# Load figures of a list scheduler, and the place from which it counts sums that need ScalarE's last copy

## The chip, the core and the metric

The kernel runs on one core of a Trainium2 chip. The time is device time of one launch in microseconds. The core's engines work side by side: TensorE (PE; its weight loads are listed as PEld), VectorE (DVE), ScalarE (ACT), GpSimd (POOL) and SyncE (SP, which issues most transfers). Each engine takes its instructions in the order in which the program emits them, and waits where an operand isn't ready or a buffer isn't free. The order of emission is therefore the schedule.

## The reference

Two blocks follow one another. The first is a gated linear recurrence over 768 steps, for 4 batches of 8 heads with head size 48:

```
f = 1 / (1 + exp(-f_logit))
for t in range(768):
    state = f[t][:, None] * state + outer(k[t], v[t])
    y[t] = q[t] @ state
```

The second takes its result as 3072 tokens of 384 channels through a bilinear layer: `((x @ w_a) * (x @ w_b)) @ w_out`, with 1536 columns in `w_a` and `w_b`. Everything is float32; the weights arrive as 64-bit numbers and are converted on the chip.

## The kernel before

**Units and blocks.** The attention is cut into 16 units: a batch, a half of the sequence (384 steps), and four heads. Two units make one block of 384 tokens (8 blocks, numbered 0 to 7). A unit's *front* (`front_parts`) prepares its inputs: two sigmoids on ScalarE (`opposite`, `sigmoid`), `affine` on POOL, and on VectorE two long scans (`scan_f`), two tiny operations (`hold`, `restart`), six short scans (`scan_inv`) and two products (`times`). Its *core* (`core_parts`) is matmuls on TensorE (`scores`, `turn`, `gains`, `within`, `across`), with `mask`, `carry` and `hand_on` on VectorE and `turned` and `out_of_bank` on ScalarE between them. The result is stored into a block's `xT` by transfers.

**The bilinear layer.** Blocks 0 and 1 use plain products (`up`: 12 chunks per block, each of 6 matmuls called beats; `product` multiplies the two halves). Blocks 2 to 7 use a scheme with fewer products over sums of weights and of `xT`: `up_triples` runs four rounds `j` of 15 products in each block. Each product of a round takes one beat on TensorE and is written to one of four PSUM banks (`ps_f`). ScalarE's `copy` or VectorE's `add` takes it out, and the bank is then used again. The third argument of `on` is the number of beats after which that happens, the *due*. In a round VectorE also does two longer sums over earlier copies (into `c[:, :, 1:3, 1]` from `first`, into `c[:, :, 0]` from `second`), and in `finish` the product of the two factors. `down` then multiplies pairs of token groups with `w_out`: 21 beats per pair. `combine_x` makes a block's sums of `xT`.

**The order up to some 111 us** is written out by hand: fronts and cores of units 0 to 3, the weights' conversion, and the first 19 chunks of `up`, which count beats as they are emitted (`on_pe`). Here the load figures play no role.

**From there a list scheduler** emits everything. `main` is a fixed list: the last ten chunks of `up`, then `down` and `up_triples` block by block. Each entry names its engine, a load in ns and a due. Beside it stand six *lines* of work in a fixed order each: sums of `w_out`, sums of `xT` (`for_x`), the attention's core, its fronts, its loads, and sums of the other weights. Before each entry of `main`, `fill` puts in whatever steps of the lines fit. It keeps a planned time `now` for TensorE and `free_at` for the other engines. A step on TensorE fits when its inputs are ready by `now`; a step on another engine when its planned start is at most one BEAT ahead of `now` and `delays` doesn't object:

```
start = max(start, free_at[engine])
fits = start <= now + BEAT and not delays(engine, start, load)
```

`delays` walks through the next 80 entries of `main` and is to say whether the step would make one of them miss its due beat. `starts` holds the planned starts of the coming beats, by a count (`beats_done`) that begins at zero with `main`; the dues were made with `beats[0]`. After a filler, `free_at[engine]` (or `now`) moves by its load. After an entry of `main` on another engine it becomes `max(free_at, now + 200) + load`.

Other limits: `across` of a new block waits in the list until the block two before it is through (`past`), since there are two `xT`; a stored unit counts as landed after 5000 ns, a load after 6000.

Of the kernel before, what the change touches and what calls it, by code (L numbers as in the profile page):

```python
# [133 lines left out]
def by_quotients(ctx, tc, q, k, f_logit, v, moe_w_a, moe_w_b, moe_w_out, out, ident, weights, bad):  # L134
# [156 lines left out]
    def front_parts(u):  # L291

        t = sets[u % NSET]
        x = halves(t["f"])
        F = halves(products_of_f[u])
        inv = invs[u % 2 if u < 2 * NQ else 0]
        none = zero.broadcast_to((128, BLK))
        got = {}

        def sigmoid():  # L300
            nc.scalar.activation(F, x, AF.Sigmoid)

        def opposite():
            nc.scalar.activation(inv, x, AF.Sigmoid, bias=less, scale=-1.0, accum_out=tails[:, u:u + 1])  # L304

        def affine():
            nc.gpsimd.tensor_scalar(inv, inv, EXP_K, 1.0, ALU.mult, ALU.add)  # L307

        def scan_f(n):
            c = slice(n * BLK, n * BLK + BLK)  # L310
            nc.vector.tensor_tensor_scan(F[:, c], F[:, c], none, math.exp(MIDDLE), ALU.mult, ALU.add)  # L311

        def hold():
            nc.vector.tensor_tensor(held[:, u], products_of_f[u][:, :, BLK - 1], least, ALU.is_ge)

        def restart():
            got["start"] = sb2.tile([128, 2, NC - 1], FP32, tag="start", name="start")
            by_chunk = products_of_f[u].rearrange("p n (c m) -> p n c m", m=C)
            nc.vector.reciprocal(got["start"], by_chunk[:, :, 0:NC - 1, C - 1])

        def scan_inv(n, c):
            w = slice(n * BLK + c * C, n * BLK + c * C + C)
            first = got["start"][:, n, c - 1:c] if c else math.exp(-MIDDLE)
            nc.vector.tensor_tensor_scan(inv[:, w], inv[:, w], none[:, 0:C], first, ALU.mult, ALU.add)  # L324

        def times(nm, by):
            live.setdefault(u, {})
            nc.vector.tensor_tensor(halves(t[nm]), halves(t[nm]), by, ALU.mult)

        first = ((ACT, 980, opposite), (ACT, 850, sigmoid))  # L330
        return (
            [*(first[::-1] if u in FIRST else first), (POOL, 1000, affine)],
            [(DVE, 870, scan_f, 0), (DVE, 870, scan_f, 1), (DVE, 160, hold)],
            [(DVE, 170, restart), *((DVE, 410, scan_inv, n, c) for n in range(2) for c in range(NC))],
            [(DVE, 880, times, "q", F), (DVE, 880, times, "k", inv)],
        )

# [222 lines left out]
        return groups[:, first:first + NTG].rearrange("p g (k t) -> p g k t", k=NFT)  # L560


    BEAT = 4 * 164
    ISSUE = 430
    beats = [0]

    def on_pe(load, do, *args):
        beats[0] += 1
        return PE, load, 0, do, *args

    def on(engine, load, due, do, *args):
        return engine, load, beats[0] + due if due else 1 << 30, do, *args

    factors = []

# [120 lines left out]
        write(b22, b22, -1)  # L696
        yield

    X_STEPS = [(DVE, 480)] + [(DVE, 270)] * 10 + [(ACT, 350)]

    def add_steps(to, x, y, op=ALU.add):
        nc.vector.tensor_tensor(to, x, y, op)  # L702
# [1 line left out]
    def up_triples(blk):  # L704
# [15 lines left out]
            return on_pe(BEAT, emit, ps, name, j, start)  # L720

        def copy(due, x, ps):
            return on(ACT, 490, due, nc.scalar.copy, x, ps)

        def finish(j, c, out, v):
            yield times(v, "v6", j)
            yield copy(5, out[1, 0], v)
            a, b = (
                c[:, g].rearrange("p k i t -> p k (i t)").rearrange("p k (g t) -> p g k t", g=NTG) for g in range(2)
            )  # L730
            yield on(DVE, 1280, 0, add_steps, to.rearrange("p g (k j) t -> p j g k t", k=NI)[:, j], a, b, ALU.mult)

        for j in range(NJ3):
            v, u, r, t = (ps_f[i][:, 0:BLK].rearrange("p (g t) -> p g t", g=2) for i in free)
            free[:] = [free[i] for i in ((2, 1, 3, 0) if j < NJ3 - 1 else (2, 3, 1, 0))]
            c = (sums, last[:, 0:2 * NI * BLK])[j % 2].rearrange("p (g k i t) -> p g k i t", g=2, k=NI, i=2)
            out = {(k, i): c[:, :, k, i] for k in range(NI) for i in range(2)}
            if j % 2:
                at = thirds.index(down_first[0])
                pairs = [thirds[(at + n) % 3] for n in (1, 2)]  # L740
            else:
                pairs = [last[:, PIECE * n:PIECE * n + PIECE] for n in range(2)]
            first, second = (x.rearrange("p (g n t) -> p g n t", g=2, n=2) for x in pairs)

            def add(due, k, i, ps):
                return on(DVE, 480, due, add_steps, out[k, i], ps, out[k, i])

            yield times(v, "v1", j, True)
            yield copy(3, out[2, 0], v)
            if tail:  # L750
                yield from finish(*tail)
            yield times(u, "u1", j, True)
            yield copy(3, out[1, 1], u)
            yield times(r, "r2", j, True)
            yield add(6, 1, 1, r)
            yield times(v, "v2", j)
            yield copy(3, out[2, 1], v)
            yield times(u, "u2", j)
            yield copy(3, first[:, :, 1], u)
            yield times(t, "t1", j, True)  # L760
            yield copy(6, out[0, 0], t)
            yield times(v, "v3", j)
            yield copy(3, first[:, :, 0], v)
            yield on(DVE, 880, 0, add_steps, c[:, :, 1:3, 1], c[:, :, 1:3, 1], first)
            yield times(u, "u3", j)
            yield copy(3, out[0, 1], u)
            yield times(r, "r3", j, True)
            yield add(6, 2, 1, r)
            yield times(v, "v4", j)
            yield copy(3, second[:, :, 1], v)  # L770
            yield times(u, "u4", j)
            yield add(3, 0, 0, u)
            yield times(t, "t2", j)
            yield add(5, 0, 1, t)
            yield times(v, "v5", j)
            yield copy(2 if j == NJ3 - 1 else 3, second[:, :, 0], v)
            yield times(u, "u5", j)
            yield add(3, 2, 0, u)
            yield on(DVE, 880, 0, add_steps, c[:, :, 0], c[:, :, 0], second)
            tail = j, c, out, v  # L780
        yield from finish(*tail)

# [2 lines left out]
    def down(pair):  # L785
# [56 lines left out]
            nc.sync.dma_start(out=out[blk * BLK + g * 128:blk * BLK + g * 128 + 128], in_=got["o", i])  # L842

        yield from times(x0, a11, b11, True)
        yield on(ACT, 330, 4, begin)
        s1, s2 = block(), block()
        yield add(10, s1, a21, a22)
        yield add(7, s2, s1, a11, ALU.subtract)
        yield from times(m1, s3, t3, True)
        yield on(ACT, 330, 7, second)  # L850
        yield from times(x0, a12, b21)
        yield on(ACT, 330, 7, third)
        s4 = block()
        yield add(10, s4, a12, s2, ALU.subtract)
        yield from times(x1, s2, t2, True)
# [11 lines left out]
    def core_parts(s):  # L867


        u = s - 1  # L870
        if u < 2 * NQ:
            yield PE, 1150, 0, scores, s, None
        elif s < NU:
            yield PE, 1850, 0, within_and_scores, u
        else:
            yield PE, 1050, 20 * BEAT, within, u
        if s < NU:
            yield DVE, 880, 0, mask, s
            yield PE, 700, 0, turn, s, None
            yield ACT, 850, 0, turned, s  # L880
        if u < 2 * NQ:
            yield PE, 1050, 0, gains, s, False
        elif s < NU:
            yield PE, 1750, 0, gains_and_across, u
        else:
            yield PE, 1050, 0, across, u, False
        if s < NU:
            for j in range(NJ - 1 if unit(s)[1] == NH - 1 else NJ):
                yield DVE, 230, 0, carry, s, j
            if unit(s)[1] < NH - 1:  # L890
                yield DVE, 500, 0, hand_on, s
        if u >= 2 * NQ:
            for part in range(3):
                yield ACT, 490, 0, out_of_bank, u, part
            begin, *stores = stores_of(u)
            yield SP, 0, 0, begin
            for do in stores:
                yield SP, ISSUE, 5000, do

# [33 lines left out]
    with tc.manual_schedule():  # L933
# [187 lines left out]
                    past=behind[blk - 1] if blk > 2 else behind["down"],  # L1121
                )

        LATENCY = 200
        now, free_at, done = 0, [0] * 5, 0

        def earliest(line):
# [8 lines left out]

        def delays(engine, start, load):

            with_it, without = start + load, free_at[engine]
            t, beat = now, beats_done  # L1140
            starts, later = {}, []
            for e, cost, due, *_ in main[done:done + 80]:
                if e == PE:
                    beat += 1
                    starts[beat] = t
                    t += cost
                elif e == engine:
                    later.append((t + LATENCY + (0 if due < 1 << 29 or e != DVE else 600), cost, due))
            for ready, cost, due in later:
                if ready >= with_it:  # L1150
                    return False
                with_it, without = (max(x, ready) + cost for x in (with_it, without))
                if with_it + 500 > max(starts.get(due, 1 << 30), without + 500):
                    return True
            return False

# [40 lines left out]
        for done, (engine, load, due, do, *args) in enumerate(main):  # L1197
# [6 lines left out]
                now += load  # L1204
                beats_done += 1
            else:
                free_at[engine] = max(free_at[engine], now + LATENCY) + load
            do(*args)  # L1208
        done = len(main)
        for line in lines:  # L1210
# [349 lines left out]
```

## Time and profile before

| what | value |
|---|---|
| median of 3 runs | 611.31 us (610.23 to 612.02) |
| profiled execution | 612.79 us, span 611.1 us |
| TensorE busy / its weight loads | 572.6 us (94%) / 511.6 us (84%) |
| VectorE busy | 410.5 us (67%) |
| ScalarE busy | 268.7 us (44%) |
| POOL busy | 76.1 us (12%) |
| mean granted TensorE clock | 0.98 |
| 240 records of products without a stall (one block of triples) | 39.24 us |

The page gives busy time per engine, the span in 40 slices, the chain that ended last, and groups of instructions with busy time, mean duration, and idle time before them with who ended it. A matmul of float32 is recorded twice, so a beat of `up_triples` shows as four records. Reported durations on VectorE and ScalarE overlap: the next instruction on the same engine can start before the reported end of the one before it. In the views of waits a line reads "engine, tile and line, waited for <- whom: us in total, times, longest us". L1208 is the scheduler's own call, under which ScalarE's copies of `main` appear; L702 is `add_steps`.

### The profile page before, as it was taken

Reading aid. Unit: us, or ns where it says so; the run is one execution under the profiler, and the core shown is the slowest. Engines: PE = TensorE matmul, PEld = TensorE weight load, DVE = VectorE, ACT = ScalarE, POOL = GpSimd, SP = SyncE. Lnnn points to the kernel's source line nnn. Section 1 sums busy time; section 2 is a strip of 40 time slices with the busy share of each in tenths; the row PEclk is TensorE's granted clock in tenths of the full one; section 3 lists DMA queues with packets and bytes.
Section 4 is the critical chain, followed back from the end, with each engine's and each line's share of the span. In section 5 each row is a group of like instructions: output and inputs, shape, how many; then the busy total and the mean of one; then the engine's idle time right before and its main releaser. Section 6 shows DMA issues by size and latency. Waiting matters only on the chain.

```text
span 611.1 us, 13867 instructions
## 1 busy us (share of the span) xinstructions
PE 572.6 (94%) x5778; PEld 511.6 (84%) x5778; DVE 410.5 (67%) x762; ACT 268.7 (44%) x508; POOL 76.1 (12%) x69
## 2 busy tenths in 40 slices
PE   0759899999999999999999999999999999999995
PEld 0626555556999999999889998999899999999995
DVE  6778434578987778976897668756776255836741
ACT  5657498963312545335531353326331245235300
POOL 6333154544200000000000000000000000000000
PEclk9859999999999999999999999999999999999998
DMA  9978586139944144034003510023001100000000
GB/s 203 241 213 251 133 268 206 53 58 164 161 124 124 37 88 92 9 106 100 20 2 81 134 34 1 2 73 72 1 3 47 35 11 1 1 27 0 1 28 31
DMA packets 33336, 49.42 MB, mean 81 GB/s; under 512 B 3952, under 2 KB 25072, under 8 KB 33264
## 3 DMA queue, kind: packets, MB, share of 16 engines
q1 hardware_dynamic: 29984, 42.38, 25.6%
q0 software_dynamic: 2992, 5.77, 5.6%
q8 instruction: 47, 0.77, 0.5%
q10 hardware_dynamic: 288, 0.30, 0.2%
q14 instruction: 25, 0.20, 0.1%
HBM read 33.23 MB, written 4.72 MB: 62 GB/s over the span
## 4 chain that ended last, share of the span: by engine, by line
PE 82%; DVE 5%; DMA 5%; ACT 2%; issue 2%; SPq 1%; ACTq 0%; DVEq 0%
PE ps_f L710 32%; PE ps_f L803 27%; PE ps_f L588 15%; DMA xT<-y 2%; PE ps_y L476 2%; PE ps_y L497 2%; PE ps_x L433 2%; PE ps_x L374 1%; DVE groups L702 1%; PE ps_x L409 1%; DMA f_in<-in_f_logit_dram 1%; DVE sums L702 1%; DMA k_in<-in_k_dram 1%; DVE inv L324 1%; DVE f_in L311 1%
## 5 line engine op out<-in xcount | busy, mean ns | idle before, releaser
L588 PE MATMUL ps_f<-xT,w_ba 128*128 128x384 f32 x288 | 99.6, 505 | 7.0 <-DMA xT<-y 3.7
L588 PEld LDWEIGHTS ps_f<-xT,w_ba 128*128 128x128 f32 x288 | 55.1, 195 | 47.0 <-issue 7.4
L1208 ACT COPY sums<-ps_f 128x384 f32<-128x384 f32 x120 | 57.6, 481 | 75.3 <-PE ps_f L710 68.7
L1208 ACT COPY groups<-ps_f 128x384 f32<-128x384 f32 x120 | 57.7, 481 | 68.4 <-PE ps_f L710 47.8
L710 PE MATMUL ps_f<-xT,w_ba 128*128 128x192 f32 x384 | 78.5, 327 | 0.0
L710 PEld LDWEIGHTS ps_f<-xT,w_ba 128*128 128x128 f32 x384 | 64.7, 190 | 0.3
L710 PE MATMUL ps_f<-x_sums,raw 128*128 128x192 f32 x288 | 53.7, 330 | 2.6 <-DVE groups L702 2.0
L710 PE MATMUL ps_f<-groups,w_ba 128*128 128x192 f32 x288 | 55.6, 328 | 0.0
L710 PEld LDWEIGHTS ps_f<-x_sums,raw 128*128 128x128 f32 x288 | 47.0, 190 | 5.5 <-DVE groups L702 3.2
L803 PE MATMUL ps_f<-w_out,groups 128*128 128x192 f32 x288 | 51.6, 328 | 0.0
L803 PE MATMUL ps_f<-w_out,sums 128*128 128x192 f32 x288 | 51.5, 327 | 0.0
L803 PE MATMUL ps_f<-spare,sums 128*128 128x192 f32 x288 | 49.8, 327 | 0.0
L710 PEld LDWEIGHTS ps_f<-groups,w_ba 128*128 128x128 f32 x288 | 47.9, 190 | 0.8 <-ACT sums L1208 0.4
L803 PEld LDWEIGHTS ps_f<-w_out,groups 128*128 128x128 f32 x288 | 47.2, 190 | 0.6
L60 POOL TENSOR_SCALAR sums<-sums 128x768 f32<-128x768 f32 (+1 forms) x20 | 41.3, 2067 | 50.8 <-ACT sums L58 49.0
L803 PEld LDWEIGHTS ps_f<-w_out,sums 128*128 128x128 f32 x288 | 47.4, 190 | 0.2
L702 DVE TENSOR_TENSOR sums<-sums,groups 128x768 f32<-128x768 f32 x36 | 35.3, 980 | 18.0 <-ACT groups L1208 17.6
L803 PEld LDWEIGHTS ps_f<-spare,sums 128*128 128x128 f32 x288 | 47.0, 190 | 0.1
L702 DVE TENSOR_TENSOR sums<-ps_f,sums 128x384 f32<-128x384 f32 x60 | 33.0, 553 | 20.0 <-PE ps_f L710 16.2
L307 POOL TENSOR_SCALAR inv<-inv 128x768 f32<-128x768 f32 x14 | 12.3, 881 | 267.0 <-ACT inv L304 241.4
L710 PE MATMUL ps_f<-x_sums,w_ba 128*128 128x192 f32 x192 | 39.6, 329 | 1.0 <-DVE groups L702 0.5
L710 PE MATMUL ps_f<-xT,raw 128*128 128x192 f32 x192 | 39.8, 330 | 0.2 <-ACT groups L1208 0.2
(123 smaller groups left out, 856.1 us busy)
## 6 DMA issues: line engine op xcount, KB each, us to landing
raw<-w_ba POOLq DMA_DIRECT2D x11, 512.0 KB, 8.2
q_in<-in_q_dram SPq DMA_DIRECT2D x32, 144.0 KB, 4.2
k_in<-in_k_dram SPq DMA_DIRECT2D x32, 144.0 KB, 3.6
v_in<-in_v_dram SPq DMA_DIRECT2D x16, 288.0 KB, 5.0
raw<-in_moe_w_out_dram SPq DMA_DIRECT2D x6, 768.0 KB, 4.2
out_dram<-o SPq DMA_DIRECT2D x24, 192.0 KB, 1.9
f_in<-in_f_logit_dram SPq DMA_DIRECT2D x28, 144.0 KB, 3.0
xT<-y SPq DMA_DIRECT2D x46, 72.0 KB, 2.1
```

The lines of the kernel that those rows point to most:

```text
L60: nc.gpsimd.tensor_scalar(h, h, HI_MAX, None, ALU.min)
L307: nc.gpsimd.tensor_scalar(inv, inv, EXP_K, 1.0, ALU.mult, ALU.add)
L311: nc.vector.tensor_tensor_scan(F[:, c], F[:, c], none, math.exp(MIDDLE), ALU.mult, ALU.add)
L324: nc.vector.tensor_tensor_scan(inv[:, w], inv[:, w], none[:, 0:C], first, ALU.mult, ALU.add)
L433: nc.tensor.matmul(ps_x[R * h:R * h + D, p, (n * NC + c) * D:(n * NC + c) * D + D], lhsT=kT[r, n, c, R * h:R * h + D], rhs=t["v"][r, n, c, ...
L476: nc.tensor.matmul(ps[p][e:e + D, o:o + SUB], lhsT=t["v"][r, n, c, h * D:h * D + D], rhs=at[r, h, o:o + SUB], start=o == 0, stop=True, ski ...
L497: nc.tensor.matmul(ps[p][e:e + D, o:o + SUB], lhsT=st[j][r, n], rhs=qf[r, tokens(n, c, p)], start=False, stop=True, skip_group_check=True,)
L588: nc.tensor.matmul(ps[nm][:, 0:BLK], lhsT=w[:, kt, ft * 128:ft * 128 + 128], rhs=xT[blk][:, kt], start=kt == 0, stop=kt == NKT - 1,)
L702: nc.vector.tensor_tensor(to, x, y, op)
L710: nc.tensor.matmul(ps[:, g], lhsT=sums_of_w[name][:, g, 128 * j:128 * j + 128], rhs=sums_of_x[blk][name], start=start and g == 0, stop=Tru ...
L803: nc.tensor.matmul(to, lhsT=x[:, i // 2, i % 2], rhs=w[:, NI * (i % 2) + i // 2], start=start and i == 0, stop=i == HFT - 1, skip_group_ch ...
L1208: do(*args)
```

## The change

It replaces load figures, and it marks entries of `main` on VectorE that read ScalarE's last copy. The mark adds 8 to the engine's number. For such an entry the main loop counts `free_at` from `last_copy + 200` where that is later than `now + 200`; `last_copy` is the planned end of the last copy emitted from `main` (before, it was set to 0 and not used). `delays` gets the same count for coming entries, in place of 600 ns on VectorE's entries that have no due. No instruction is added or removed, and no instruction's operands change.

```
-        first = ((ACT, 980, opposite), (ACT, 850, sigmoid))
+        first = ((ACT, 930, opposite), (ACT, 750, sigmoid))
-            [*(first[::-1] if u in FIRST else first), (POOL, 1000, affine)],
-            [(DVE, 870, scan_f, 0), (DVE, 870, scan_f, 1), (DVE, 160, hold)],
-            [(DVE, 170, restart), *((DVE, 410, scan_inv, n, c) for n in range(2) for c in range(NC))],
+            [*(first[::-1] if u in FIRST else first), (POOL, 830, affine)],
+            [(DVE, 870, scan_f, 0), (DVE, 870, scan_f, 1), (DVE, 80, hold)],
+            [(DVE, 90, restart), *((DVE, 385, scan_inv, n, c) for n in range(2) for c in range(NC))],
...
-    BEAT = 4 * 164
+    BEAT = 653
+    COPIED = 8
...
-    def on(engine, load, due, do, *args):
-        return engine, load, beats[0] + due if due else 1 << 30, do, *args
+    def on(engine, load, due, do, *args, copied=False):
+        return engine + COPIED * copied, load, beats[0] + due if due else 1 << 30, do, *args
...
-            return on(ACT, 490, due, nc.scalar.copy, x, ps)
+            return on(ACT, 400, due, nc.scalar.copy, x, ps)
...
-            yield on(DVE, 1280, 0, add_steps, to.rearrange("p g (k j) t -> p j g k t", k=NI)[:, j], a, b, ALU.mult)
+            yield on(DVE, 1280, 0, add_steps, to.rearrange("p g (k j) t -> p j g k t", k=NI)[:, j], a, b, ALU.mult, copied=True)
...
-            yield add(6, 1, 1, r)
+            yield add(6, 1, 1, r, True)
...
-            yield on(DVE, 880, 0, add_steps, c[:, :, 1:3, 1], c[:, :, 1:3, 1], first)
+            yield on(DVE, 870, 0, add_steps, c[:, :, 1:3, 1], c[:, :, 1:3, 1], first, copied=True)
...
-            yield on(DVE, 880, 0, add_steps, c[:, :, 0], c[:, :, 0], second)
+            yield on(DVE, 870, 0, add_steps, c[:, :, 0], c[:, :, 0], second, copied=True)
...
-            yield PE, 1850, 0, within_and_scores, u
+            yield PE, 1600, 0, within_and_scores, u
...
-            yield PE, 700, 0, turn, s, None
-            yield ACT, 850, 0, turned, s
+            yield PE, 850, 0, turn, s, None
+            yield ACT, 700, 0, turned, s
...
-            yield PE, 1750, 0, gains_and_across, u
+            yield PE, 1550, 0, gains_and_across, u
...
-                yield DVE, 230, 0, carry, s, j
+                yield DVE, 180, 0, carry, s, j
-                yield DVE, 500, 0, hand_on, s
+                yield DVE, 320, 0, hand_on, s
...
-        LATENCY = 200
+        LATENCY, MARGIN = 200, 500
...
-            with_it, without = start + load, free_at[engine]
+            with_it, without, copied = start + load, free_at[engine], max(free_at[ACT], last_copy)
...
-                elif e == engine:
-                    later.append((t + LATENCY + (0 if due < 1 << 29 or e != DVE else 600), cost, due))
+                    continue
+                ready = t + LATENCY
+                if e >= COPIED:
+                    ready = max(ready, copied + LATENCY)
+                if e == ACT:
+                    copied = max(ready, copied) + cost
+                if e % COPIED == engine:
+                    later.append((ready, cost, due))
...
-                if with_it + 500 > max(starts.get(due, 1 << 30), without + 500):
+                if with_it + MARGIN > max(starts.get(due, 1 << 30), without + MARGIN):
...
-                free_at[engine] = max(free_at[engine], now + LATENCY) + load
+                ready = max(now, last_copy if engine >= COPIED else 0) + LATENCY
+                engine %= COPIED
+                free_at[engine] = max(free_at[engine], ready) + load
+                if engine == ACT:
+                    last_copy = free_at[ACT]
```

Smaller figures change in the same way: `scores`, `within`, `gains` and `across` alone to 1000, adds in the rounds from 480 to 470, three small copies in `down` from 330 to 220, the first and last step of `combine_x` from 480 and 350 to 470 and 270.

More of the change, by code (lines that the diff above doesn't have):

```diff
@@ L697, in combine_x @@
         yield
-    X_STEPS = [(DVE, 480)] + [(DVE, 270)] * 10 + [(ACT, 350)]
+    X_STEPS = [(DVE, 470)] + [(DVE, 270)] * 10 + [(ACT, 270)]
     def add_steps(to, x, y, op=ALU.add):
@@ L743, in up_triples, with add @@
             first, second = (x.rearrange("p (g n t) -> p g n t", g=2, n=2) for x in pairs)
-            def add(due, k, i, ps):
-                return on(DVE, 480, due, add_steps, out[k, i], ps, out[k, i])
+            def add(due, k, i, ps, copied=False):
+                return on(DVE, 470, due, add_steps, out[k, i], ps, out[k, i], copied=copied)
             yield times(v, "v1", j, True)
@@ L844, in down @@
         yield from times(x0, a11, b11, True)
-        yield on(ACT, 330, 4, begin)
+        yield on(ACT, 220, 4, begin)
         s1, s2 = block(), block()
@@ L849, in down @@
         yield from times(m1, s3, t3, True)
-        yield on(ACT, 330, 7, second)
+        yield on(ACT, 220, 7, second)
         yield from times(x0, a12, b21)
-        yield on(ACT, 330, 7, third)
+        yield on(ACT, 220, 7, third)
         s4 = block()
@@ L871, in core_parts @@
         if u < 2 * NQ:
-            yield PE, 1150, 0, scores, s, None
+            yield PE, 1000, 0, scores, s, None
         elif s < NU:
-            yield PE, 1850, 0, within_and_scores, u
+            yield PE, 1600, 0, within_and_scores, u
         else:
-            yield PE, 1050, 20 * BEAT, within, u
+            yield PE, 1000, 20 * BEAT, within, u
         if s < NU:
             yield DVE, 880, 0, mask, s
-            yield PE, 700, 0, turn, s, None
-            yield ACT, 850, 0, turned, s
+            yield PE, 850, 0, turn, s, None
+            yield ACT, 700, 0, turned, s
         if u < 2 * NQ:
-            yield PE, 1050, 0, gains, s, False
+            yield PE, 1000, 0, gains, s, False
         elif s < NU:
-            yield PE, 1750, 0, gains_and_across, u
+            yield PE, 1550, 0, gains_and_across, u
         else:
-            yield PE, 1050, 0, across, u, False
+            yield PE, 1000, 0, across, u, False
         if s < NU:
             for j in range(NJ - 1 if unit(s)[1] == NH - 1 else NJ):
-                yield DVE, 230, 0, carry, s, j
+                yield DVE, 180, 0, carry, s, j
             if unit(s)[1] < NH - 1:
-                yield DVE, 500, 0, hand_on, s
+                yield DVE, 320, 0, hand_on, s
         if u >= 2 * NQ:
```

## The prediction

> **What bounds the kernel now.** I read the page's busy rows first, then its groups, then the table by stretches of 25 us, then the waits of TensorE's weight loads and of VectorE between 195 and 485 us, then the timeline of VectorE around single stalls.
>
> From the page:
>
> ```profile
> PE 572.6 (94%) x5778; PEld 511.6 (84%) x5778; DVE 410.5 (67%) x762; ACT 268.7 (44%) x508; POOL 76.1 (12%) x69
> PE 0759899999999999999999999999999999999995
> ...
> L1208 ACT COPY sums<-ps_f 128x384 f32<-128x384 f32 x120 | 57.6, 481 | 75.3 <-PE ps_f L710 68.7
> ```
>
> TensorE is the bound: a nine in nearly every slice from 75 us on. The planner orders work from about 111 us (its first 10 chunks of `up`, 3.9 us each, end at 151 us). Everything before has a fixed order, and from 485 us on only the main list runs, whose own order is fixed. So the change can act only between about 111 and 485 us. From the table by stretches (PE, PEld, DVE, ACT, POOL busy):
>
> ```profile
> 300.00:325.00 25.00, 23.80 (x307) 21.89 (x306) 22.83 (x45) 9.77 (x22) 0.83 (x1) 1.00 0.01 2
> ...
> 350.00:375.00 25.00, 23.87 (x227) 22.01 (x226) 18.76 (x30) 11.95 (x25) 0.83 (x1) 1.00 0.15 35
> ...
> 550.00:575.00 25.00, 25.00 (x156) 25.00 (x155) 15.73 (x22) 12.26 (x26) 0.00 (x0) 1.00 0.00 1
> ```
>
> The last row is a stretch of products alone: weight loads without a gap, clock 1.00. The first two hold attention work and stalls.
>
> **The ceiling, and a first rule weighed.** By the PE row, all waits for VectorE and ScalarE from 195 to 485 us are 2.6+0.7+0.6+0.4 = 4.3 us. The Trainium skill (Perfetto Trace Analysis, "Identifying the Most-Contended Engine") says that matmul occupancy is a poor measure of headroom, since matmuls are pipelined, and that the busy share of the weight loads is better. The waits of the weight loads:
>
> ```profile
> PEld ps_f L710 <- DVE groups L702: 4.6, 7, 1.2
> ...
> PEld ps_f L710 <- ACT groups L1208: 1.7, 5, 0.5
> ...
> PEld ps_f L710 <- DVE sums L702: 1.3, 2, 0.7
> PEld ps_f L710 <- ACT sums L1208: 1.2, 5, 0.3
> PEld ps_x L409 <- DVE at L397: 0.9, 1, 0.9
> ```
>
> VectorE releases 4.6+1.3+0.9 = 6.8 us, ScalarE 1.7+1.2 = 2.9 us: 9.7 us. By the one view the most to be won is 4.3 us, by the other 9.7. I take the second, lowered to 8.7, since about 0.1 us of the first weight load at each of the roughly ten long stalls would be visible anyway. That is 1.4% of the run.
>
> **Why these stalls are there.** A bank of `ps_f` wanted "3 beats" after its product is wanted two beats (2 x 0.65 = 1.31 us) after that product ended. The add takes 0.55 and the hand-over 0.05, so it must start within 0.7 us. The planner puts a front piece on VectorE when its planned start is at most one beat (0.65) ahead, so an add may be planned at 0.65+0.87 = 1.52 us. `delays` should forbid this, but it compares due beats with a count that starts at zero when the main list starts, while `beats` has already counted 6 beats for each of the 19 chunks emitted by `up` before: 114. It looks 80 lines ahead, so it never finds the due beat, uses 1<<30, and never says no. VectorE at one stall (starts in the first column):
>
> ```profile
> 428.05 0.54 DVE L702 TENSOR_TENSOR groups<-ps_f,groups 128x384 f32<-128x384 f32 x1
> 428.50 0.48 DVE L324 TENSOR_TENSOR_SCAN inv<-inv,start,zero 128x128 f32<-128x128 f32 x1
> 428.89 0.40 DVE L324 TENSOR_TENSOR_SCAN inv<-inv,zero 128x128 f32<-128x128 f32 x1
> 429.20 0.53 DVE L702 TENSOR_TENSOR groups<-ps_f,groups 128x384 f32<-128x384 f32 x1
> ```
>
> Two scans stand ahead of the add at 429.20; the next weight load starts at 429.79, 0.68 us late. The starts also show real intervals: a scan holds VectorE 0.31 or 0.39, an add 0.45.
>
> **The change, part by part.**
>
> *`delays`, MARGIN.* With the due never found, the new body also always lets through: 0. If a due were found, this would be a new guard, which I leave to the range.
>
> *Sums behind the last copy.* This works through the main loop's `free_at`. Before, such a sum is counted from now+0.20. Now it is counted from last_copy+0.20, and a copy emitted just before ends at now+0.20+0.40: now+0.80, so 0.60 later when the queues are empty. Only the `first` sum and `finish`'s product follow their copy directly; `add(6,1,1)` and the `second` sum come a beat (0.65) later, by which time the copy is over: 0. In blocks 2 to 5 that is 4 x 4 x 2 = 32 sums. How many really waited, in the view of waits from 195 to 485 us:
>
> ```profile
> DVE groups L702 <- ACT sums L1208: 14.1, 11, 2.0
> ...
> DVE sums L702 <- ACT groups L1208: 8.9, 9, 2.4
> ...
> DVE sums L702 <- ACT sums L1208: 2.5, 1, 2.5
> DVE groups L702 <- ACT groups L1208: 2.5, 2, 1.5
> ```
>
> That is 28.0 us in 23 waits which the count left out. Behind a waiting sum stand, in VectorE's order, the fillers placed there and then the bank-clearing adds, for which TensorE waits. The change counts 23 x 0.60 = 13.8 us of them, so fewer fillers are put between sum and add. No row gives TensorE's price of a late VectorE; I take the ratio of the views, 6.8 us of stall to 28.0 us of waiting = 0.24. Gain 13.8 x 0.24 = 3.3 us. Ends: 0, if fillers only change places, and 6.8, if every stall VectorE causes goes.
>
> *VectorE's loads.* A front was counted 2x870+160+170+6x410+2x880 = 6290 and is now 2x870+80+90+6x385+2x880 = 5980. By the intervals it takes about 1730+80+90+2x310+4x385+1720 = 5780. So 0.31 us of padding goes per front. That padding hid part of the uncounted waits, so 12 fronts x 0.31 x 0.24 = 0.9 us lost. `carry` and `hand_on` were padded too (counted 0.23 each and 0.25 by their row, about 0.18 from start to start); they run in a burst behind TensorE, beside products: within the range.
>
> *TensorE's loads.* `within_and_scores` takes 0.82+0.73 = 1.55 us in the chain and was counted 1.85, now 1.60. `gains_and_across` takes 0.69+0.67 = 1.36, was 1.75, now 1.55. `turn` takes 0.66, was 0.70, now 0.85. Overcounted time makes the planner think that VectorE has drained: 0.30+0.39+0.04 = 0.73 before, 0.05+0.19+0.19 = 0.43 after. 12 units x 0.30 x 0.24 = 0.9 us won. The two load terms cancel. BEAT 653 for 656 is the measured 0.65: 0.
>
> *ScalarE's loads, and a second rule weighed.* Back to back, a copy occupies ScalarE about 0.37 though the row says 481. The skill (Perfetto Trace Analysis, "DVE / Act Engine Instruction (TENSOR_ADD, Activation, etc)") says that an instruction signals only at its reported end, after the write is acknowledged; the next one on its own engine may start earlier. So 400 is right for ScalarE's queue and 0.08 short for whoever reads the copy. That speaks against the change. By the rule each copy that clears a bank would be planned 0.08 to 0.09 too early: 12 units at 0.09 are 1.1 us, and the sum would be -2.2. By the rows, the sums get 0.40+0.20 = 0.60, which covers 481 and the hand-over, and ScalarE is 44% busy, so its queue is mostly empty: 0. I take 0 and keep 1.1 for the range. Its cover is that idle time; where a sigmoid pair stands ahead of a copy it is gone, and ScalarE's 2.9 us of stalls are such places.
>
> *POOL, SP.* `affine` 1000 to 830 lets the second scans be planned 0.17 earlier; its row says 0.88. No transfer is added. Loads and stores follow their steps: stores are planned at 5.0 us and land in 2.1, loads at 6.0 and land in 3 to 5. The cover is the wait of `across` for a free block of `xT`, several us per block. Without it a late unit would hold a whole block: 0 here.
>
> **Sum.** -3.3+0.9-0.9 = -3.3 us. The profiled execution took 612.8 (span 611.1 and 1.7 around it): it becomes 609.5. Against the median 611.31, which is 1.5 lower, 608.0.
>
> **Rivals.** About 0.3% (1.8 us) is what a measurement here can tell from no change.
> - *The stalls only move* (0.19): `delays` is still inert and the limit of one beat is the same, so each chain of scans still runs VectorE full, as at 428 us where no ScalarE wait stands ahead. 611 us, 609.5 to 613.1.
> - *Nearly all of VectorE's stalls go* (0.20), as the counted order now matches: -5.3 to -8.7, 602.6 to 606. Against it: stalls like that at 429.
> - *Slower* (0.13): without padding the planner fills VectorE to its true limit inside triple blocks 2 to 5. Each front queues 0.31 us deeper ahead of an add, and where the queue is full that passes to TensorE whole: 12 x 0.31 = 3.7, less about 0.9 for TensorE's loads: 614.1. It decides once the copied sums win less than 1 us, that is when fewer than 7 of the 23 keep a filler away.
> - The likeliest case (0.48) is a partial gain, 606 to 609.4.
>
> **How the numbers follow.** Faster 0.48+0.20 = 0.68, same 0.19, slower 0.13. The range 603.8 to 613.8 leaves out the lower part of the second rival (about 0.07) and the upper half of the third (about 0.07). The likeliest case's own range is 606 to 609.4.
>
> **What would show it.** Right: VectorE's 28.0 us of waiting for ScalarE falls below 20, more front pieces stand ahead of a copied sum, and the weight loads' waits fall from 9.7 to about 6. The stretches 485 to 604 us keep their length. Wrong: waits of L710 for VectorE stay at 6 us or more, or those for ScalarE pass 4. The prediction falls if stalls at chains of scans grow, or if a block of sums of `xT` starts late.

## The result and the profile after

The changed kernel takes 607.75 us (median of 7 runs, 607.0 to 610.89) beside 611.47 us for the kernel before on the same chips: a ratio of 0.9951, interval 0.993 to 0.9973. That is 3.7 us less by the medians, 3.0 by the ratio and 1.7 to 4.3 by its interval; forecast were 3.3 less and 608.0.

The page of the changed kernel (its line numbers are one higher: L711 is the former L710, L703 the former L702; L1219 is the former L1208):

```profile
span 607.6 us, 13865 instructions
## 1 busy us (share of the span) xinstructions
PE 572.1 (94%) x5778; PEld 512.0 (84%) x5778; DVE 408.7 (67%) x762; ACT 268.8 (44%) x508; POOL 74.9 (12%) x69
```

All busy times are the same as before within 2 us, and the number of operations on each engine is the same. So the work has not changed; waiting of TensorE has gone. The waits of the weight loads from 195 to 485 us show where:

```profile
PEld ps_f L711 <- DVE groups L703: 2.1, 4, 1.0
PEld ps_f L711 <- ACT groups L1219: 1.4, 5, 0.5
...
PEld ps_f L711 <- DVE sums L703: 1.1, 3, 0.6
PEld ps_x L433 <- ACT sums L1219: 0.7, 3, 0.2
PEld ps_f L711 <- ACT sums L1219: 0.5, 2, 0.3
PEld ps_f L804 <- DVE o L839: 0.3, 1, 0.3
PEld ps_f L804 <- DVE u L833: 0.2, 1, 0.2
```

VectorE releases 2.1+1.1+0.3+0.2 = 3.7 us where it released 6.8. ScalarE releases 1.4+0.7+0.5 = 2.6 us where it released 3.3 (the prediction's 2.9, and two waits of 0.2 at `ps_x` L433 that it left out; all waits of the two engines before are thus 10.1 us, not 9.7). The planner also works from 111 to 195 us, and there the changed kernel has waits that the kernel before lacks:

```profile
PEld ps_x L433 <- ACT x_sums L609: 0.5, 1, 0.5
PEld ps_f L804 <- DVE groups L611: 0.4, 1, 0.4
PEld ps_x L433 <- ACT u L819: 0.2, 1, 0.2
```

So some 2.7 us of waiting are gone in all, nearly all of it VectorE's. The two stretches that were worst before, in the table by stretches (PE, PEld, DVE, ACT, POOL busy):

```profile
300.00:325.00 25.00, 24.29 (x227) 23.07 (x226) 22.79 (x47) 8.78 (x20) 0.00 (x0) 1.00 0.03 7
350.00:375.00 25.00, 24.65 (x235) 23.34 (x234) 18.79 (x31) 12.88 (x28) 0.83 (x1) 1.00 0.15 36
```

The weight loads are busy 23.07 and 23.34 us of 25, where they were 21.89 and 22.01.

**How two profiles are compared here.** The part written out by hand has the same order in every kernel of this study, yet its long run of products starts anywhere between 72.2 and 76.1 us. So I measure from the start of that run to the start of block 6's triples, and call this the *planned stretch*, though its first 35 us or so still belong to the part written by hand. It is read from two lines of the chain. For the kernel before:

```profile
75.98 66.11 PE ps_f L588 x204
...
485.01 39.24 PE ps_f L710 x240
```

and for the changed kernel:

```profile
74.76 66.19 PE ps_f L589 x204
...
481.38 39.24 PE ps_f L711 x240
```

That is 409.03 us before and 406.62 after: 2.4 us less, in one execution of each. The spans differ by 3.5 us; the other 1.1 is the start (75.98 against 74.76, 1.2 us), which the change doesn't touch. From block 6's triples to the end both take 126.1 to 126.2 us.

### The profile page after: what moved, and what is told of

Same layout as the page of the kernel before. It is cut to its first block, busy times and chain, and to the rows that moved or that the text cites. A ratio compares the mean times of both kernels' runs of the same rounds, so it can differ in the third digit from the quotient of the medians.

```text
span 607.6 us, 13865 instructions
## 1 busy us (share of the span) xinstructions
PE 572.1 (94%) x5778; PEld 512.0 (84%) x5778; DVE 408.7 (67%) x762; ACT 268.8 (44%) x508; POOL 74.9 (12%) x69
## 4 chain that ended last, share of the span: by engine, by line
PE 83%; DVE 5%; DMA 4%; ACT 2%; issue 2%; SPq 1%; ACTq 0%; DVEq 0%
PE ps_f L711 34%; PE ps_f L804 27%; PE ps_f L589 14%; DMA xT<-y 2%; PE ps_y L497 2%; PE ps_x L433 2%; PE ps_y L476 2%; PE ps_x L374 2%; DVE groups L703 1%; DMA q_in<-in_q_dram 1%; DVE sums L703 1%; DMA raw<-in_moe_w_a_dram 1%; PE ps_x L409 1%; DVE inv L324 1%; SPq L208 1%
## 5 line engine op out<-in xcount | busy, mean ns | idle before, releaser
L1219 ACT COPY sums<-ps_f 128x384 f32<-128x384 f32 x120 | 57.4, 480 | 75.5 <-PE ps_f L711 67.9
L1219 ACT COPY groups<-ps_f 128x384 f32<-128x384 f32 x120 | 57.7, 481 | 63.1 <-PE ps_f L711 41.1
L711 PE MATMUL ps_f<-xT,w_ba 128*128 128x192 f32 x384 | 78.4, 327 | 0.0
L711 PEld LDWEIGHTS ps_f<-xT,w_ba 128*128 128x128 f32 x384 | 64.8, 190 | 0.2
L711 PE MATMUL ps_f<-groups,w_ba 128*128 128x192 f32 x288 | 55.7, 328 | 0.0
L711 PE MATMUL ps_f<-x_sums,raw 128*128 128x192 f32 x288 | 54.0, 331 | 1.2 <-DVE groups L703 0.9
L711 PEld LDWEIGHTS ps_f<-x_sums,raw 128*128 128x128 f32 x288 | 46.9, 190 | 4.2 <-DVE groups L703 2.1
L711 PEld LDWEIGHTS ps_f<-groups,w_ba 128*128 128x128 f32 x288 | 47.8, 190 | 0.7 <-ACT groups L1219 0.6
L703 DVE TENSOR_TENSOR sums<-sums,groups 128x768 f32<-128x768 f32 x36 | 34.7, 964 | 14.2 <-ACT groups L1219 13.7
L703 DVE TENSOR_TENSOR sums<-ps_f,sums 128x384 f32<-128x384 f32 x60 | 32.9, 552 | 16.6 <-PE ps_f L711 15.0
L711 PE MATMUL ps_f<-x_sums,w_ba 128*128 128x192 f32 x192 | 39.3, 327 | 0.3 <-DVE sums L703 0.3
L711 PE MATMUL ps_f<-xT,raw 128*128 128x192 f32 x192 | 39.5, 328 | 0.0
```

The source lines that it names most:

```text
L711: nc.tensor.matmul(ps[:, g], lhsT=sums_of_w[name][:, g, 128 * j:128 * j + 128], rhs=sums_of_x[blk][name], start=start and g == 0, stop=Tru ...
```

## The experiments

Each ratio is to runs of the kernel before made beside it, whose median was 611.38 us for e1 to e4, 611.64 for e5 to e8 and 611.79 for e9 to e12. A planned stretch is one execution.

| run | what | time, us | ratio (interval) | planned stretch, us |
|---|---|---|---|---|
| | before | 611.47 | 1 | 409.03 |
| | changed | 607.75 | 0.9951 (0.993 to 0.9973) | 406.62 |
| e1 | mark alone | 607.51 | 0.9934 (0.9919 to 0.995) | 404.38 |
| e2 | all loads, no mark | 612.18 | 1.0011 (1.0001 to 1.002) | 409.69 |
| e3 | POOL's load alone | 611.05 | 0.999 (0.9979 to 1.0002) | 409.09 |
| e4 | changed, guard repaired | 603.45 | 0.9878 (0.9856 to 0.9899) | 400.99 |
| e5 | VectorE's loads alone | 611.05 | 0.9994 (0.9984 to 1.0003) | 408.03 |
| e6 | TensorE's loads alone | 610.24 | 0.9981 (0.997 to 0.9991) | 407.82 |
| e7 | changed, copy at 490 | 608.83 | 0.9958 (0.9942 to 0.9975) | 406.18 |
| e8 | before, guard repaired | 603.25 | 0.9863 (0.9843 to 0.9883) | 401.09 |
| e9 | changed, half a beat | 606.40 | 0.9914 (0.9892 to 0.9935) | 403.76 |
| e10 | mark, guard repaired | 602.63 | 0.9859 (0.9837 to 0.988) | 400.38 |
| e11 | e4 with margin 750 | 603.61 | 0.9879 (0.9857 to 0.9901) | 400.89 |
| e12 | loads, guard repaired, no mark | 604.60 | 0.9881 (0.9857 to 0.9905) | 401.07 |

(In e10 the block that stands as one piece in the chain is block 7's, at 527.79; block 6's 39.24 and a `down` of 13.65 us are taken off, then the start at 74.52.)

### e1: the mark alone

All load figures are as before; of the change it holds the marks, the edit of `delays`, and in the main loop:

```
+                ready = max(now, last_copy if engine >= COPIED else 0) + LATENCY
+                engine %= COPIED
+                free_at[engine] = max(free_at[engine], ready) + load
+                if engine == ACT:
+                    last_copy = free_at[ACT]
```

> All load figures as in the kernel before; only the sums that need ScalarE's last copy are counted behind it. Theory (the prediction's step): this mark alone brings the gain, since the load terms cancel: about 608 us, VectorE's waits for ScalarE clearly below 28 us. Rival (the loads bring it): 611, no change. Rival (the gain is only the luck of a reshuffled order): any value from 608 to 613, with no fall in those waits.

607.51 us, ratio 0.9934: the mark alone brings 3.1 to 5.0 us, no less than the whole change. That is the theory's number, and it speaks against the loads as the cause, which e2 settles. But one half of the expectation failed. VectorE's waits for ScalarE from 195 to 485 us did not fall, which was also the sign set for a mere reshuffle of the list:

```profile
DVE sums L703 <- ACT groups L1219: 12.8, 9, 2.6
...
DVE groups L703 <- ACT sums L1219: 11.3, 10, 1.7
...
DVE groups L703 <- ACT groups L1219: 3.1, 3, 1.7
...
DVE sums L703 <- ACT sums L1219: 2.8, 1, 2.8
```

Together 30.0 us, against 28.0 before. What fell is what TensorE pays for them, in the waits of the weight loads:

```profile
PEld ps_f L711 <- ACT groups L1219: 1.8, 6, 0.6
...
PEld ps_f L711 <- ACT sums L1219: 1.1, 5, 0.3
PEld ps_f L711 <- DVE sums L703: 0.9, 2, 0.5
PEld ps_f L711 <- DVE groups L703: 0.8, 2, 0.6
```

VectorE releases 1.7 us where it released 6.8; ScalarE, with 0.5 us more at `ps_x` L433, 3.4 where it released 3.3. The timeline shows how. VectorE before, at one sum that waits for ScalarE (start, duration, engine and line; in brackets the idle time before; the last line is the weight load that waits):

```profile
232.80 0.96 DVE L702 TENSOR_TENSOR sums<-sums,groups 128x768 f32<-128x768 f32 x1 [1.28 <-ACT groups L1208]
233.68 0.95 DVE L311 TENSOR_TENSOR_SCAN f_in<-f_in,zero 128x384 f32<-128x384 f32 x1
234.55 0.53 DVE L702 TENSOR_TENSOR sums<-ps_f,sums 128x384 f32<-128x384 f32 x1
235.00 0.95 DVE L311 TENSOR_TENSOR_SCAN f_in<-f_in,zero 128x384 f32<-128x384 f32 x1
235.86 1.00 DVE L702 TENSOR_TENSOR sums<-ps_f,sums 128x384 f32<-128x384 f32 x2
...
236.45 0.79 PEld L710 LDWEIGHTS ps_f<-x_sums,raw 128*128 128x128 f32 x5 [0.59 <-DVE sums L702]
```

With the mark and this kernel's load of 490 for a copy, the count has VectorE free 0.69 us later at such a sum. Without it the planner put a scan (0.87 us from start to start) directly behind the sum, and another behind the one add that follows. The add at 235.86, the first of two, releases TensorE 0.59 us late. VectorE in e1, at the same place:

```profile
232.30 0.96 DVE L703 TENSOR_TENSOR sums<-sums,groups 128x768 f32<-128x768 f32 x1 [0.89 <-ACT groups L1219]
233.37 0.56 DVE L703 TENSOR_TENSOR sums<-ps_f,sums 128x384 f32<-128x384 f32 x1
233.84 0.95 DVE L311 TENSOR_TENSOR_SCAN f_in<-f_in,zero 128x384 f32<-128x384 f32 x1
234.71 1.00 DVE L703 TENSOR_TENSOR sums<-ps_f,sums 128x384 f32<-128x384 f32 x2
```

The sum still waits (0.89), but the add comes first and the scan behind it, and the next adds start at 234.71. Of the long sums of VectorE that waited more than 0.15 us for ScalarE between 195 and 485 us, 8 of 22 had a filler directly behind them in the kernel before, 2 of 21 in e1, and 3 of 19 in the changed kernel. So the mark works by keeping fillers from behind a waiting sum, not by filling the wait.

A stall need not follow at once. The one at 429.79, which the prediction shows, stands at the end of a run of scans and adds that began 7 us earlier behind a waiting product of `finish`, and VectorE was not idle in between. The kernel before:

```profile
422.75 1.36 DVE L702 TENSOR_TENSOR groups<-sums 128x1152 f32<-128x1152 f32 x1 [0.98 <-ACT sums L1208]
424.03 0.95 DVE L311 TENSOR_TENSOR_SCAN f_in<-f_in,zero 128x384 f32<-128x384 f32 x1
```

e1:

```profile
418.98 1.36 DVE L703 TENSOR_TENSOR groups<-sums 128x1152 f32<-128x1152 f32 x1 [1.71 <-ACT sums L1219]
420.25 0.55 DVE L703 TENSOR_TENSOR groups<-ps_f,groups 128x384 f32<-128x384 f32 x1
```

With the mark the add comes before the scans. Where TensorE waited 0.68 and 0.63 us for VectorE in this run of the kernel before, it does not wait for it in e1, only once for ScalarE (0.6 us).

Two of the four marks do nothing by themselves: e1 without the marks on `add(6, 1, 1)` and on the `second` sum emits exactly the same order, as the prediction's "a beat later: 0" says.

### e2: the loads without the mark

```
-                ready = max(now, last_copy if engine >= COPIED else 0) + LATENCY
+                ready = now + LATENCY
```

> All load figures as in the changed kernel; the main loop counts a marked sum as it did before. Theory: the loads on VectorE cost about 0.9 us and those on TensorE win about 0.9, so about 611.3. Rival (the loads bring the gain): 607.5 to 608.5. The rival that less padding fills VectorE deeper ahead of the adds: 612 to 614.

612.18 us, ratio 1.0011: a loss of 0.1 to 1.2 us. The loads don't bring the gain. The waits of the weight loads for VectorE are 5.8+1.3 = 7.1 us, as many as before:

```profile
PEld ps_f L711 <- DVE groups L703: 5.8, 6, 1.4
...
PEld ps_f L711 <- DVE sums L703: 1.3, 4, 0.7
```

### e3: a figure that should be worth nothing

```
-            [..., (POOL, 1000, affine)],
+            [..., (POOL, 830, affine)],
```

> The kernel before with one figure changed, affine on POOL counted 830 for 1000. POOL's real time and VectorE's count are untouched, so as a mechanism it is worth 0 and only reshuffles the list (about 60 of VectorE's 640 planned entries change places). Theory: within 1 us of 611.3. Rival (any reshuffle moves the time by some us): more than 1.8 us either way.

611.05 us, ratio 0.999, interval on both sides of 1. About 60 of VectorE's entries change places, and the time moves by 0.3 us by the medians and 0.6 by the ratio. One such draw doesn't prove that no reshuffle can move the time. But e2, e5 and e6 are draws too, and all four lie between 1.8 us faster and 1.2 us slower, ends of intervals included. That speaks against luck as the source of 4 us.

### e4 and e8: the guard repaired

```
-        beats_done, last_copy = 0, 0
+        beats_done, last_copy = beats[0] - sum(e == PE and do is not check_held for e, _, _, do, *_ in main), 0
```

The count of beats then starts at the 114 already used, and `delays` finds the due beats. e4 is this in the changed kernel, e8 in the kernel before.

> The changed kernel with the count of beats that delays uses set to the 114 beats already counted, so that due beats are found and fillers that would make an add or copy late are held back. Theory (stalls come from fillers that the dead guard lets through): weight loads wait under 3 us for VectorE and ScalarE, 603 to 606. Rival (held-back fillers pile up and a unit comes late, or stalls only move): 607 or more. If the guard had worked all along, nothing would change: 607.8.

> The kernel before with the count of beats repaired and nothing else. Theory (most stalls come from fillers in front of adds that the dead guard lets through): 604 to 606, weight loads wait about 3 us. If the mark on the sums is needed for the guard to be right, this stays 2 us or more above the 603.5 of the changed kernel with the same repair; if the guard alone does it, within 1 us.

603.45 and 603.25 us: 7.9 and 8.4 us less than the kernel before, about twice what the change brings, and for e8 more than expected. The repair alone, with the old loads and no mark, does as well as with both. The waits of the weight loads of e8, from 195 to 485 us:

```profile
PEld ps_x L433 <- ACT groups L1208: 0.9, 4, 0.2
PEld ps_f L803 <- DVE u L832: 0.7, 1, 0.7
PEld ps_f L710 <- ACT sums L1208: 0.5, 2, 0.3
PEld ps_f L710 <- DVE sums L702: 0.4, 1, 0.4
```

The stalls at VectorE's adds are nearly gone, though of 23 long sums that waited for ScalarE in e8, again 8 have a filler directly behind them. So such a filler is no cost by itself; it costs where the add behind it is due. In e4 the two worst stretches have PE busy in full:

```profile
300.00:325.00 25.00, 25.00 (x321) 24.17 (x320) 22.66 (x47) 7.58 (x16) 0.83 (x1) 1.00 0.05 17
350.00:375.00 25.00, 25.00 (x243) 24.69 (x242) 22.16 (x38) 13.04 (x28) 0.83 (x1) 1.00 0.07 17
```

VectorE has no less to do there than before (22.66 and 22.16 us busy, where it was 22.83 and 18.76).

### e5 and e6: two load terms apart

e5 has only VectorE's figures of the change (but for the long sums, which stay at 880), e6 only TensorE's:

```
-            [(DVE, 870, scan_f, 0), (DVE, 870, scan_f, 1), (DVE, 160, hold)],
+            [(DVE, 870, scan_f, 0), (DVE, 870, scan_f, 1), (DVE, 80, hold)],
...
-            yield PE, 1850, 0, within_and_scores, u
+            yield PE, 1600, 0, within_and_scores, u
```

> The kernel before with VectorE's load figures alone changed (scans, hold, restart, carry, hand_on, adds). Theory (the prediction's term): less padding costs about 0.9 us, 612.2. Rival (the padding was worth what the queue says): 614 to 615. Rival (no systematic effect): 610.5 to 612.

> The kernel before with TensorE's load figures alone changed (BEAT, scores, within, turn, gains, across). Theory (the prediction's term): wins about 0.9 us, 610.4. Rival (no effect): 611 to 612. If TensorE's figures and VectorE's cancel, this run and the one of VectorE's figures lie on two sides of 611.4 by about as much.

e6 is 1.2 us faster by its ratio (0.9981, interval 0.6 to 1.8), near the forecast 0.9. e5 is not slower: 0.9994, between 1.0 us faster and 0.2 slower. So the two terms don't cancel; VectorE's padding hid nothing that shows.

### e7: the rule on reported ends

```
-            return on(ACT, 400, due, nc.scalar.copy, x, ps)
+            return on(ACT, 490, due, nc.scalar.copy, x, ps)
```

> The changed kernel with ScalarE's copy in the rounds counted 490 again (the reported duration) in place of 400 (start to start). Theory (the sums' 0.20 of latency covers the reported end): within 0.5 us of the changed kernel's 607.8. Rival (the rule that a reader on another engine waits for the reported end): about 1.1 us faster, 606.7.

0.9958 (0.9942 to 0.9975), beside 0.9951 for the changed kernel: no difference that this shows. The median is 1.1 us longer, outside the half us that was expected, and the planned stretch 0.4 us shorter. The two intervals leave anything open from 1.2 us faster to 2.1 slower, so they don't quite exclude the rival's 1.1. The rule itself, that a reader on another engine waits for the reported end, agrees with the trace. In the kernel before, the copy in front of the waiting sum shown under e1 is

```profile
232.29 0.48 ACT L1208 COPY groups<-ps_f 128x384 f32<-128x384 f32 x1
```

It ends by its record at 232.77, and the sum starts at 232.80. From the start of the copy to the start of its reader are thus 0.48+0.03 = 0.51 us, and the planner counts 0.40+0.20 = 0.60 even with the shorter figure. That this cover is why 0.09 us more change nothing is likely, but not shown.

### e9: a shallower queue

```
-                        fits = start <= now + BEAT and not delays(engine, start, load)
+                        fits = start <= now + 326 and not delays(engine, start, load)
```

> The changed kernel, guard still dead, but a filler fits only when its planned start is at most half a beat (0.33 us) ahead of TensorE, not one. Theory (the depth of the queue that the planner allows sets the stalls): an add is planned at most 0.33 later, so VectorE's stalls fall by about half of the 3.2 us that are left, 605.5 to 607. Rival (depth doesn't matter, only what the guard would see): 607 to 609. Rival (work piles up behind): over 609.

606.40 us, within the theory's range. The weight loads' waits for VectorE are 0.6 us in all; ScalarE's are left:

```profile
PEld ps_f L711 <- ACT sums L1219: 1.4, 4, 0.6
...
PEld ps_x L433 <- ACT sums L1219: 0.7, 3, 0.2
PEld ps_f L711 <- ACT groups L1219: 0.5, 1, 0.5
PEld ps_f L711 <- DVE sums L703: 0.4, 1, 0.4
...
PEld ps_f L711 <- DVE groups L703: 0.2, 1, 0.2
```

So in the changed kernel the depth to which the planner may queue fillers sets VectorE's stalls. It still gives 403.76 us for the planned stretch where the live guard gives 401: what else the guard saves there was not taken apart.

### e10, e11, e12: what is left with a live guard

e10 is e1 with the repair, e12 is e2 with it, and e11 is e4 with one figure more:

```
-        LATENCY, MARGIN = 200, 500
+        LATENCY, MARGIN = 200, 750
```

> The kernel before with the repaired count of beats and the mark on the sums, old load figures. Theory (the mark and the guard remove the same stalls): within 0.7 us of the 603.3 that the repaired count alone gave. If the two add up: 600 to 601.5.

> The changed kernel's load figures with the repaired count, main loop without the mark. Theory (a live guard makes both parts of the change idle): within 0.7 us of 603.3. If exact loads matter once the guard reads them: 601 to 602.5.

> The changed kernel with the repaired count and a margin of 750 for 500. Theory: what stalls are left with the repaired count (2.5 us, all released by ScalarE) come from copies planned too close to their due beat, so a wider margin takes half of them: 602 to 603. Rival (they are fixed by the order of the main list itself): 603 to 604.

Ratios 0.9859, 0.9881 and 0.9879 in this order, with intervals of about 0.002 to each side: all the kernels with a live guard lie together. The two parts of the change are worth nothing that shows once the guard works, so mark and guard do not add up: they remove largely the same stalls, by different means. (e12's median, 604.60, is above what was expected, though its ratio is not apart from the others, and its planned stretch, 401.07, is that of e8.) A wider margin takes nothing away: e11 missed the 602 to 603 of its theory, and its rival, that the stalls left are fixed by the order of the main list, came in with 603.61. That order itself was not varied. e10, the kernel before with the mark and the repair, has the lowest median of the study: 602.63 us, 1.4% less than before.

## Why the prediction was right

**The ceiling, and the choice of view.** By PE's own row no more than 4.3 us could be won between 195 and 485 us. e4, e8 and e10 won 7.5 to 8.6 us by their ratios, and the planned stretch of e10 is 8.65 us shorter. The rule that the prediction takes from the Trainium skill (Perfetto Trace Analysis, "Identifying the Most-Contended Engine") decided rightly here, and the planned stretches of before and e10 show why (length, then PE and PEld busy):

```profile
75.98:485.01 409.03, 404.69 (x4222) 360.83 (x4223) 291.15 (x549) 182.87 (x349) 47.93 (x35) 1.00 0.32 78
```

```profile
74.52:474.90 400.38, 400.38 (x4180) 361.67 (x4181) 289.11 (x550) 183.88 (x347) 48.81 (x35) 1.00 0.33 79
```

For the same products PE's row is busy 4.3 us less, while the weight loads differ by 0.8 (some records are missing from a trace). So half of what was won had been counted as busy by PE's row. The granted clock is 1.00 in both. The number 8.7, however, was met by luck. e10 still has 2.2 us of waits for VectorE and ScalarE from 195 to 485 us, so 7.9 of the 10.1 us went and 8.65 were won. The sum of these waits is close to what can be won, but no exact bound, and taking 0.1 us off for each long stall finds no support in what was won.

**The mark: 3.3 us forecast, 3.1 to 5.0 measured (e1).** The place was right: the count at sums behind a copy. So was the step "fewer fillers are put between sum and add" (8 of 22 before, 3 of 19 after), and the weight loads' waits fell to 6.3 us where about 6 were forecast. That the size came out is in part luck. It was 28.0 us of waiting, counted at 0.60 for each of 23 waits, times a stall of 0.24 for each us of waiting. That ratio is not a property of the kernel: in e1 it is 1.7 to 30.0, or 0.06. Two signs set for being right also failed. "VectorE's 28.0 us of waiting for ScalarE falls below 20": in e1 it is 30.0, in the changed kernel 13.8+5.0+1.3 = 20.1. "More front pieces stand ahead of a copied sum": directly ahead of such sums stand 32 in the changed kernel, 37 before. The waiting is no cost by itself, since VectorE has time. What costs is a filler in front of an add that is due.

**`delays` at 0.** Right by the code: the dues lie 114 beats past its count and it looks 80 entries ahead, so it can't object in either kernel, and the edits to it, MARGIN among them, were without effect. What this was worth shows in e8, where the repaired count takes 1.4% off the time.

**The load terms: one right, one wrong.** TensorE's 0.9 us won was 1.2 (e6). VectorE's 0.9 us lost was not there (e5). By the prediction the two were to cancel. All loads together lose 0.1 to 1.2 us (e2), while POOL's (e3, not clear of noise), VectorE's and TensorE's alone win 0.6, 0.4 and 1.2 by the middle of their intervals. If the parts added up, ScalarE's figures would cost 2 to 3 us. They were not run alone; e7 gives no sign that it is the copy's figure, though only to within 1.2 us and with the mark in place. This stays open. A list scheduler's parts needn't add up, since each changes what the others find. So that the forecast sum came out is luck in this part: a loss was expected from VectorE's figures that isn't there, and one from elsewhere was not expected.

**The rivals.** "The stalls only move" falls: VectorE's went from 6.8 to 3.7 us, and ScalarE's did not grow. Its example, the stall at 429 "where no ScalarE wait stands ahead", was misread: one stands 7 us ahead, and with the mark alone that stall is gone (e1). "Nearly all of VectorE's stalls go" is not what the change did, but e9 came near it (0.6 us), and so did e1 (1.7). "Slower" rested on padding passing whole to TensorE, which e5 excludes.

**ScalarE.** Taken as 0. Its stalls went from 3.3 to 2.6 us between 195 and 485 us, and 0.5+0.2 us came in before 195: 0 in the end, and e7 doesn't argue for another value.

## What to carry to other kernels

Before refining figures in a planner, see whether its checks ever fire: here a count that began at zero in one place and at 114 in another made the guard blind, and one line of repair was worth twice the whole retuning. In a queue that keeps its order an instruction that waits cost nothing here until something urgent stood behind it (30.0 us of waiting in e1, 1.7 us of stall), so count the wait and look at what is queued after it. Read the headroom of TensorE from its weight loads: its own busy row would have put the limit here at half of what was then won.

## What was not expected of the hardware

Part of the scatter is made at the start. In the profiles of this study the first long run of products begins between 72.2 and 76.1 us, though everything before it is emitted in the same order, while a block of triples takes 39.24 us in every profile whose chain shows block 6 in one piece. Which transfer at the start makes the difference was not followed up. Differences of one or two us between single profiles of this kernel are therefore read from the planned stretch, not from the spans.
